# A new order for every engine of a clustered-attention and gated-FFN kernel, with some casts and copies on other engines and other PSUM banks

## The chip, the core and the metric

One core of a Trainium2 chip runs the whole kernel. The metric is the time of one execution on the device in microseconds (us); of several runs the median is given. The engines of the core are TensorE (PE, with its weight loads as PEld), VectorE (DVE), ScalarE (ACT), GpSimd (POOL) and SyncE (SP), which here only issues DMAs. Each engine works through its own queue in order.

## What is computed

Four batches, eight heads, 768 tokens, 64 columns a head. Each query and each key is given the cluster (of 16) whose normalized centroid it is closest to. A query attends only to the keys of its own cluster, and the output of the attention goes through a gated FFN with a convolution of three taps over the tokens:

```python
mask = q_assign[:, :, :, None] == k_assign[:, :, None, :]
scores = where(mask, scale * q @ k.T, -1e9)
x = softmax(scores) @ v                       # heads side by side: 4 x 768 x 512
h = maximum(x @ w_in, 0.0)                    # 1024 columns
conv_out = sum(conv_w[k] * hp[:, k:k + S, :] for k in range(3))
out = (h * sigmoid(conv_out)) @ w_out         # 4 x 768 x 512, float32
```

## The kernel before

The work is written as a list of some 1,680 short steps, the string `PLAN`. The function `step` (line 752) turns each into instructions, in the order of the list; no scheduler moves them afterwards. So the list fixes the order of every engine's queue, and a step waits on its engine until its operands are there and the buffers that it writes are free. A suffix such as `@2` names the PSUM bank that a matmul step writes: 0 to 3 are the four `flex` banks, 4 and 5 are the two halves of the score buffer `sc0` (used so only at the end).

The heads are taken in pairs, `g` = 0 to 15, four pairs to a batch. The attention runs in 32 slots `t`, one for a pair and half of its queries (384); a pair has two slots. The steps, by name:

- **Loads.** `L`, `LQ`, `LK`, `LZ`, `LV` load queries, keys and values (SP's queue; `La` on ACT's), `_wl` weights. Pairs 0 to 6 are transposed on PE (`T`, line 301) and copied out of PSUM by ACT (`Qa`) or DVE (`Qd`); pairs 7 to 15 are transposed in blocks on DVE (`Z`).
- **Casts to 16 bits.** `CD` (POOL), `CDd` (DVE), `CDa` (ACT) write queries and keys into `ext`, `CV` and `CVd` the values, `_wp`, `_wd`, `_wa` the weights. `_z` and `_zd` clear the other half of `ext`. They all go through `copy` (line 319), so most of them show as line 323 (POOL and DVE) or 321 (ACT).
- **Clusters.** `A` multiplies with the centroids (line 347), `M0` to `M6` find the best one on DVE (lines 364 to 389), `K` turns the result on PE, `B` copies it on DVE (line 406) and `BX` sends it by DMA into rows of `ext`, `BA` does so from ACT's queue (line 410). For pair 0 `KM` and `KCa`/`KCd` (line 423) write these rows by copies. With these rows the score matmul adds a large negative number where the clusters differ.
- **Attention.** `S.t.i` (i = 0 to 5) are two score matmuls of 384 columns into one of two score buffers (line 442). `E.t.i` is the exponential on ACT (line 454), 128x768. `V.t.u` (u = 0 to 5) are six matmuls that add up 128 rows of the result in a `flex` bank (line 466). `N.t` divides by the sum on DVE (lines 479 and 480). The result goes to `xT` by a DMA transpose (`XD`) or by PE and a copy (`X`, `Ya`, `Yd`).
- **FFN**, for units `n` = 0 to 31 (a batch, half of the tokens, two blocks of 128 columns). `I.n.f` are four matmuls (line 524), `Ra`/`Rd` the relu (lines 537 and 539), `C`/`Ca`/`Cd` carry three columns between the halves. The convolution is three steps `c`, `a`, `b` on DVE (lines 558 and 560), or `W` on PE into a score buffer (line 566) with the taps that `_ta`, `_td`, `_tp` make. `H` is the tanh (line 584), `G` the gate on DVE (line 592).
- **Output.** `O` are two, `U` one of the eight matmuls of a 128-row output tile (line 604), `Fa`/`Fd` empty the bank (lines 617 and 619), `FX` stores.
- **Set-up.** `_k` are three matmuls of zeros; `_id`, `_io`, `_n0` to `_n7d`, `_cw0` to `_cw2`, `_pk`, `_sd`, `_v`, `_hz` make constants.

Buffers rotate: four for query and key loads, four for value loads, six for `ext`, four for `attn`, two score buffers, two for `x16`, three for `hpad`, two each for the convolution and the tanh, four for outputs.

Of the kernel before, what the change touches and what calls it, by code (L numbers as in the profile page):

```python
# [871 lines left out]
```

## Time and profile before

| | |
|---|---|
| median of 3 runs (lowest to highest) | 241.73 us (241.42 to 241.91) |
| the profiled execution | 240.68 us |
| its span, first to last instruction | 238.9 us |
| granted TensorE clock, mean | 0.998 |
| idle of PE, DVE, ACT, POOL in the span | 11.2, 23.5, 23.5, 154.3 us |

A row of a group reads: line, engine, operation, out<-in with shapes, count, then busy us and mean ns of one, then the idle time of the engine just before them with what ended it. A row of the timeline reads: start and length in us, engine, line, operation, count, and in brackets the idle time before it and what ended it. A matmul's length holds the way through the array too, so the pace of a run of matmuls is read from their starts.

### The profile page before, as it was taken

To read this page: it belongs to the slowest core of one execution; us is meant where nothing else is said; L and a number is where in the kernel's file an instruction comes from. 1 tells how busy PE (TensorE), PEld (TensorE's weight loads), DVE (VectorE), ACT (ScalarE), POOL (GpSimd) and SP (SyncE) were. 2 spreads that over 40 slices of the span, in tenths; PEclk is the share of its full clock that TensorE was granted. 3 is DMA by queue.
4 is the path that set the end of the run, shared out by engine and by line. 5 is a ranking of instruction groups with operands and counts; after the bars stand their busy time and mean duration, and the time that the engine had idled before them with its cause. 6 is when DMAs were issued, how large, how long until landed. Compare 5 with 4: busy or idle time off the path is not lost.

```text
span 238.9 us, 6438 instructions
## 1 busy us (share of the span) xinstructions
PE 227.7 (95%) x2442; PEld 143.5 (60%) x2442; DVE 215.4 (90%) x497; ACT 215.4 (90%) x337; POOL 84.6 (35%) x149
## 2 busy tenths in 40 slices
...
GB/s 198 294 243 257 157 233 245 323 80 83 242 92 136 183 128 94 173 126 183 163 150 169 114 3 188 153 134 1 168 89 63 33 47 16 105 64 112 68 0 177
DMA packets 102958, 32.77 MB, mean 137 GB/s; under 512 B 94603, under 2 KB 98187, under 8 KB 102926
## 3 DMA queue, kind: packets, MB, share of 16 engines
...
q10 hardware_dynamic: 327, 0.24, 0.4%
...
## 4 chain that ended last, share of the span: by engine, by line
PE 64%; DVE 15%; ACT 12%; POOL 5%; issue 2%; DVEq 0%; POOLq 0%
PE sc L442 17%; PE flex L524 15%; PE flex L604 14%; PE flex L466 10%; ACT attn L454 8%; PE flex L347 3%; POOL ext L323 3%; PE sc L566 3%; ACT th L584 2%; DVE best L380 1%; DVE ext L323 1%; DVE cnv L560 1%; DVE x L480 1%; PE sc L604 1%; DVE val L377 1%
## 5 line engine op out<-in xcount | busy, mean ns | idle before, releaser
L454 ACT ACTIVATE attn<-sc 128x768 f16<-128x768 f32 x192 | 146.4, 817 | 4.0 <-PE sc L442 2.7
L442 PE MATMUL sc<-ext 128*128 128x384 f16 x384 | 89.3, 325 | 3.8 <-ACT attn L454 2.1
L466 PEld LDWEIGHTS <-attn 128*128 128x128 f16 x1152 | 50.5, 97 | 15.2 <-ACT attn L454 0.4
L560 DVE SCALAR_TENSOR_TENSOR cnv<-hpad,cwcol,cnv 128x382 f16<-128x382 f16 (+1 forms) x100 | 58.4, 609 | 0.4
L323 POOL CAST ext<-qkT 64x768 f16<-64x768 f32 x48 | 41.7, 875 | 40.6 <-DVE qkT L298 20.0
L466 PE MATMUL flex<-v,attn 128*128 128x65 f16 x1152 | 54.5, 193 | 0.3 <-ACT attn L454 0.3
L524 PE MATMUL flex<-xT,w_in 128*128 128x384 f16 x256 | 49.1, 326 | 0.1
L442 PEld LDWEIGHTS <-ext 128*128 128x128 f16 x384 | 32.5, 97 | 26.9 <-issue 9.2
L604 PE MATMUL flex<-w_out,hg 128*128 128x512 f16 x176 | 47.1, 379 | 0.0
L592 DVE SCALAR_TENSOR_TENSOR hg<-th,hpad 128x764 f16<-128x764 f32 (+2 forms) x33 | 30.7, 934 | 3.1 <-ACT th L584 3.0
L524 PEld LDWEIGHTS <-w_in 128*128 128x128 f16 x256 | 23.9, 98 | 15.6 <-issue 0.6
L604 PEld LDWEIGHTS <-hg 128*128 128x128 f16 x192 | 17.9, 98 | 16.8 <-DVE hg L592 1.1
L537 ACT ACTIVATE hpad<-flex 128x384 f16<-128x384 f32 x45 | 21.8, 501 | 2.4 <-PE flex L524 1.6
L323 POOL CAST v<-v_in 128x768 f16<-128x768 f32 x15 | 14.6, 977 | 24.7 <-DMA v_in<-in_v_dram 24.6
L584 ACT ACTIVATE th<-cnv 128x764 f32<-128x764 f16 (+1 forms) x25 | 21.2, 848 | 0.7 <-DVE cnv L560 0.7
L323 POOL COPY hpad<-hf 128x6 f16<-128x6 f16 x12 | 4.9, 418 | 42.0 <-DVE hg L592 41.8
L480 DVE TENSOR_TENSOR x<-flex,rec 128x384 f16<-128x384 f32 x32 | 17.8, 558 | 1.1
L298 DVE STREAM_TRANSPOSE qkT<-qk_in 128x768 f32<-128x768 f32 x18 | 17.3, 966 | 0.0
L558 DVE TENSOR_SCALAR cnv<-hpad,cwcol 128x382 f16<-128x382 f16 (+1 forms) x50 | 16.3, 349 | 0.6 <-ACT hpad L537 0.5
L323 POOL COPY hf<-hpad 128x6 f16<-128x6 f16 x11 | 3.6, 329 | 30.7 <-ACT hpad L537 18.6
L347 PE MATMUL flex<-qkT,cT 128*32 128x192 f32 x256 | 14.1, 333 | 0.0
L309 PE MATMUL flex<-id,qk_in 128*128 128x128 f32 x84 | 12.5, 287 | 1.2 <-ACT qkT L315 0.6
...
## 6 DMA issues: line engine op xcount, KB each, us to landing
...
```

Source lines behind the costliest of these rows:

```text
L323: (nc.vector if name == "d" else nc.gpsimd).tensor_copy(out=to, in_=src)
L347: nc.tensor.matmul(bank[at][32 * j : 32 * (j + 1), 192 * i : 192 * (i + 1)], lhsT=cT32[:, which, :], rhs=tokens[:, j], start=True, stop=Tr ...
L442: nc.tensor.matmul(s[:, n, 0:HS], lhsT=ext_b[g % NE][:, h, 1, P * (kt + n) : P * (kt + n + 1)], rhs=ext_b[g % NE][:, h, 0, HS * a : HS * ( ...
L454: nc.scalar.activation(attn[t, i // 3][:, kt : kt + 2, :], sc[(6 * t + i) % 2][:, :, 0:HS], AF.Exp, scale=0.125)
L466: nc.tensor.matmul(avp(at)[:, u, 0 : D + 1], lhsT=attn[t, h][:, kt, P * jq : P * (jq + 1)], rhs=v16_b[g % NE][:, h, kt, 0 : D + 1], start= ...
L480: nc.vector.tensor_tensor(out=x16[t].rearrange("p jq (h d) -> p h jq d", h=2), in0=av[:, :, 0:D].rearrange("p (h jq) d -> p h jq d", h=2), ...
L524: nc.tensor.matmul(bank[at][:, 0:HS], lhsT=w_in16[:, r, 2 * u + f, :], rhs=xT[:, b % 2, r, HS * a : HS * (a + 1)], start=(r == 0), stop=(r ...
L537: nc.scalar.activation(to, src, AF.Relu)
L560: nc.vector.scalar_tensor_tensor(out=cnv, in0=src, scalar=w, in1=cnv, op0=ALU.mult, op1=ALU.add)
L584: nc.scalar.activation(th_t[n][:, fs, 0:N], pre[:, fs, 0:N], AF.Tanh, scale=0.5)
L592: nc.vector.scalar_tensor_tensor(out=hg_b[b][:, 2 * u + fs.start : 2 * u + fs.stop, LO[a] : LO[a] + N], in0=th_t[n][:, fs, 0:N], scalar=1. ...
L604: nc.tensor.matmul(bank[at][:, 0:Dm], lhsT=hg_b[b][:, fb, P * tq : P * (tq + 1)], rhs=w_out16[:, fb, :], start=(fb == 0), stop=(fb == NFB ...
```

## The change

The list is laid out anew: each engine's order, the engine of some casts and copies, and the banks. The kinds and counts of all matmul steps stay, except that one `_k` (three matmuls of zeros) is gone. `KR = P` slices `ext` to the 128 partitions that it has.

The steps that differ in engine, by count (before, after): ACT: `CDa` 7, 8; `KCa` 2, 1; `Qa` 16, 15; `Ra` 45, 46; `Fa` 19, 16; `Ya` 3, 2; `_ta` 9, 8; `_wa` 4, 3. DVE: `CDd` 9, 6; `CVd` 1, 2; `KCd` 2, 3; `Qd` 7, 8; `Rd` 19, 18; `Fd` 5, 8; `Yd` 2, 3; `Cd` 7, 4; `_wd` 4, 3; `_zd` 4, 5. POOL: `CD` 48, 50; `CV` 15, 14; `C` 23, 26; `_tp` 10, 11; `_wp` 8, 10; `_z` 8, 7.

133 lines of the list go and 133 come. Here are its beginning, places in the middle and its end, and the two other edits:

```diff
@@ -15,140 +15,140 @@
...
-    "LQ.0.0 _id _io _zero _k.10@2 _zd.5.0 _k.17@3 _zd.3.0 _zd.3.1 _pk.4 _sd _z.0.1 _k.14@1 _hz.1 _z.1.1 "
-    "_cent _n1 _z.1.0 _z.0.0 _hz.2 _pk.0 _v.1 _z.2.1 _pk.2 _pk.1 _z.4.0 T.0.0@2 La.0.0 T.0.1@1 _n0 _nq _n2 "
-    "_n5 _id16 _zd.4.1 _n3@3 _n4@3 Qa.0.0 Qa.0.1 CDd.0.0.1 CDa.0.0.0 LK.0.1 T.0.3@2 Qa.0.3 A.0.0@3 M0.0.0 "
-    "M1.0.0 M2.0.0 M3.0.0 _cw0 LQ.0.1 T.0.2@1 Qa.0.2 CDa.0.1.1 LQ.1.0 T.1.0@0 _cw1@2 _cw2 _tp.20 Qa.1.0 "
-    "A.0.1@1 M4.0.0 M0.0.1 M1.0.1 M5.0.0 M2.0.1 M6.0.0 M3.0.1 LK.1.0 T.1.1@3 Qa.1.1 _ta.10 CDd.1.0.0 LQ.1.1 "
-    "T.1.2@1 Qa.1.2 LK.1.1 T.1.3@0 A.1.0@2 M0.1.0 M1.1.0 Qa.1.3 CD.1.1.1 _ta.6 _td.22 KM.0.0.1@1 KCa.0.0.1 "
-    "KM.0.0.0@3 KCd.0.0.0 M4.0.1 M2.1.0 M3.1.0 M4.1.0 A.1.1@2 M0.1.1 M5.1.0 M5.0.1 M6.1.0 M6.0.1 M1.1.1 "
-    "_z.5.1 CDa.0.1.0 S.0.0 "
-    "E.0.0 L.2 T.2.0@0 Qa.2.0 T.2.2@1 Qa.2.2 T.2.1@3 Qa.2.1 CD.2.1.1 CD.1.1.0 CD.1.0.1 S.0.1 E.0.1 _n7d "
-    "M2.1.1 M3.1.1 M4.1.1 _v.0 _pk.3 CD.2.0.0 S.0.2 _tp.19 K.1.0@1 B.1.0 KM.0.1.0@2 KCd.0.1.0 E.0.2 "
-    "CDa.2.1.0 A.2@3 M0.2 M1.2 KM.0.1.1@1 KCa.0.1.1 CD.2.0.1 _tp.21 M5.1.1 _td.8 M6.1.1 M2.2 _k.3@0 L.3 "
-    "T.3.0@2 Qa.3.0 T.3.1@0 Qa.3.1 CDd.3.0.1 M3.2 _z.2.0 T.3.2@1 Qa.3.2 CD.3.1.1 CD.3.0.0 _v.3 CD.3.1.0 "
-    "S.0.3 E.0.3 S.0.4 E.0.4 K.1.1@0 B.1.1 BA.1.1 _ta.7 M4.2 M5.2 M6.2 L.4 T.4.2@3 T.4.0@2 T.4.1@1 S.0.5 "
-    "E.0.5 Qa.4.0 Qd.4.2 Qd.4.1 A.3@0 M0.3 LV.0 CV.0 BX.1.0 S.1.0 S.1.1 "
...
-    "S.4.0 T.6.1@0 Qd.6.1 V.2.5@2 K.5@3 S.4.1 "
...
-    "E.9.0 A.8@2 M0.8 N.6 S.9.2 E.9.1 E.9.2 M1.8 B.7 M2.8 S.9.3 E.9.3 V.9.0@2 S.9.4 V.9.1@2 V.9.2@2 LZ.9.0 "
-    "BX.6 LZ.9.1 Z.9.0 H.2 G.2 E.9.4 S.9.5 E.9.5 CV.4 V.8.0@1 V.8.1@1 V.8.2@1 V.8.3@1 V.8.4@1 S.10.0 "
...
-    "E.18.3 V.17.4@0 V.17.5@0 O.1.0.0@1 E.18.4 a.13.1 Rd.14.1 M4.13 N.17 b.13.1 a.12.1 a.13.0 M5.12 M5.13 "
...
-    "CV.10 V.18.0@1 V.18.1@1 O.1.1.0@3 S.19.4 V.18.2@1 V.18.3@1 M6.13 H.12 G.12 M6.12 E.19.4 V.19.0@0 S.19.5 "
...
+    "_zero _hz.2 _pk.0 _cent _zd.2.0 _zd.2.1 _z.4.1 _k.14@3 _sd _z.0.0 _id _z.1.0 _k.17@1 _k.10@3 _zd.0.1 "
+    "La.0.0 LQ.0.0 T.0.0@1 _n0 _n1 _nq _n2 _n3@2 _n5 _n4@2 T.0.1@3 Qa.0.0 Qd.0.1 _id16 CDd.0.0.1 LK.0.1 "
+    "T.0.3@2 Qa.0.3 LQ.0.1 T.0.2@0 Qa.0.2 CDa.0.0.0 A.0.0@3 M0.0.0 M1.0.0 M2.0.0 _io A.0.1@0 M0.0.1 M1.0.1 "
+    "M3.0.0 _n7d M4.0.0 M2.0.1 M5.0.0 CDa.0.1.1 LK.1.1 T.1.3@3 LQ.1.0 T.1.0@2 Qa.1.0 LK.1.0 T.1.1@1 Qa.1.1 "
+    "_pk.1 _z.5.0 CDa.0.1.0 _cw0 _cw1@2 _cw2 _tp.11 LQ.1.1 T.1.2@1 Qa.1.2 Qa.1.3 CD.1.1.0 _tp.19 M6.0.0 "
+    "KM.0.0.0@2 M3.0.1 M4.0.1 M5.0.1 A.1.0@0 M0.1.0 KCd.0.0.0 M6.0.1 M1.1.0 M2.1.0 KM.0.0.1@1 KCa.0.0.1 "
+    "CD.1.0.1 _z.3.1 A.1.1@0 M0.1.1 M3.1.0 M1.1.1 M4.1.0 M2.1.1 M5.1.0 M3.1.1 M4.1.1 _td.16 M6.1.0 CDa.1.1.1 "
+    "S.0.0 "
+    "E.0.0 L.2 T.2.0@3 Qa.2.0 T.2.2@0 Qa.2.2 KM.0.1.0@1 KCd.0.1.0 T.2.1@2 Qa.2.1 CD.2.0.1 _pk.4 _v.0 "
+    "CD.2.1.1 CD.2.0.0 S.0.1 E.0.1 KM.0.1.1@3 KCd.0.1.1 A.2@0 CDd.1.0.0 M5.1.1 S.0.2 S.0.3 K.1.0@1 B.1.0 "
+    "CDa.2.1.0 _pk.2 E.0.2 E.0.3 M0.2 M1.2 M2.2 M6.1.1 M3.2 _z.3.0 L.3 T.3.2@3 T.3.0@1 T.3.1@2 Qa.3.0 Qa.3.1 "
+    "CD.3.0.0 S.0.4 E.0.4 S.0.5 K.1.1@1 Qa.3.2 CD.3.1.1 CD.3.1.0 CD.3.0.1 _zd.1.1 B.1.1 BA.1.1 L.4 T.4.0@2 "
+    "Qd.4.0 T.4.1@0 M4.2 T.4.2@1 Qd.4.2 E.0.5 Qa.4.1 _ta.7 A.3@2 M0.3 M1.3 M5.2 M2.3 M6.2 LV.0 BX.1.0 S.1.0 "
...
+    "E.3.0 T.6.1@2 Qd.6.1 S.3.2 E.3.1 E.3.2 X.0@1 S.3.3 T.6.2@0 S.3.4 E.3.3 _wl.0 K.4@2 LV.2 CVd.2 V.2.0@3 "
+    "E.3.4 S.3.5 E.3.5 Yd.0 Qd.6.2 M3.5 M4.5 B.4 M5.5 V.2.1@3 V.2.2@3 _td.5 M6.5 _wd.14 S.4.0 V.2.3@3 S.4.1 "
+    "E.4.0 V.2.4@3 S.4.2 E.4.1 E.4.2 CDd.6.0.1 K.5@0 V.2.5@3 N.2 B.5 S.4.3 A.6@1 M0.6 _wp.0 _tp.2 S.4.4 "
...
+    "E.9.1 V.8.0@1 S.9.2 V.8.1@1 V.8.2@1 V.8.3@1 V.8.4@1 S.9.3 E.9.2 E.9.3 V.8.5@1 N.8 S.9.4 S.9.5 E.9.4 "
+    "E.9.5 V.9.0@3 V.9.1@3 S.10.0 V.9.2@3 "
...
+    "c.14.1 V.17.4@0 V.17.5@0 N.17 G.12 c.13.1 S.19.2 E.19.2 _ta.12 O.1.1.0@2 O.1.1.1@2 LV.11 LZ.14.1 S.19.3 "
+    "V.18.0@0 V.18.1@0 S.19.4 V.18.2@0 E.19.3 E.19.4 I.15.0@3 Ra.15.0 C.15 S.19.5 V.18.3@0 V.18.4@0 E.19.5 "
...
-    "E.20.0 V.19.2@0 O.1.1.1@3 V.19.3@0 S.20.1 S.20.2 V.19.4@0 XD.17 XD.18 V.19.5@0 N.19 XD.19 FX.0.3 FX.1.0 "
...
-    "V.20.0@1 V.20.1@1 S.21.1 V.20.2@1 "
...
-    "S.31.4 O.2.2.3@3 V.31.2@0 Fd.2.2 FX.2.2 E.31.3 FX.2.4 Cd.27 S.31.5 E.31.4 O.3.0.0@2 O.3.0.1@2 E.31.5 "
-    "O.3.1.0@3 V.31.3@0 V.31.4@0 V.31.5@0 O.3.1.1@3 O.3.0.2@2 O.3.0.3@2 N.31 X.31@0 Ya.31 _ta.14 O.3.1.2@3 "
-    "O.3.1.3@3 Fa.3.1 FX.3.1 Fd.3.0 FX.3.0 I.28.0@2 I.28.1@0 Ra.28.0 Rd.28.1 I.29.1@3 I.30.0@1 Ra.30.0 "
-    "I.29.0@2 Cd.28 W.28.0@1 W.28.1@1 Ra.29.0 Rd.29.1 C.26 Cd.30 c.30.0 a.30.0 b.30.0 H.28 G.28 C.25 C.29 "
-    "I.30.1@2 Ra.30.1 c.30.1 I.31.0@1 Rd.31.0 a.30.1 b.30.1 W.29.0@1 W.29.1@1 H.29 G.29 H.30 G.30 I.31.1@3 "
-    "U.3.5.0@0 U.3.5.1@0 U.3.3.0@5 U.3.3.1@5 U.3.2.0@4 C.31 W.31.0@1 U.3.4.0@1 U.3.2.1@4 U.3.3.2@5 U.3.3.3@5 "
-    "U.3.2.2@4 U.3.2.3@4 Ra.31.1 U.3.5.2@0 W.31.1@1 H.31.0 G.31.0 H.31.1 U.3.4.1@1 U.3.2.4@4 U.3.3.4@5 "
-    "U.3.4.2@1 U.3.3.5@5 U.3.2.5@4 U.3.2.6@4 G.31.1 U.3.2.7@4 Fa.3.2 FX.3.2 U.3.3.6@5 U.3.3.7@5 Fa.3.3 "
-    "FX.3.3 U.3.5.3@0 U.3.5.4@0 U.3.5.5@0 U.3.5.6@0 U.3.5.7@0 U.3.4.3@1 U.3.4.4@1 U.3.4.5@1 U.3.4.6@1 Fa.3.5 "
-    "FX.3.5 U.3.4.7@1 Fa.3.4 FX.3.4 "
...
+    "V.19.2@1 V.19.3@1 S.20.4 V.19.4@1 V.19.5@1 E.20.4 S.20.5 E.20.5 Ra.15.1 FX.1.0 XD.17 FX.0.5 LZ.15.0 "
+    "XD.18 N.19 XD.19 LV.14 A.14@3 S.21.0 V.20.0@1 S.21.1 Fd.1.1 V.20.1@1 V.20.2@1 "
...
+    "O.2.2.3@3 V.31.2@0 S.31.5 O.3.0.0@2 O.3.0.1@2 O.3.0.2@2 E.31.5 V.31.3@0 V.31.4@0 V.31.5@0 N.31 _tp.0 "
+    "O.3.1.0@1 O.3.1.1@1 O.3.1.2@1 X.31@0 Yd.31 O.3.1.3@1 Fa.3.1 O.3.0.3@2 Fd.3.0 Cd.27 XD.30 I.28.0@0 C.26 "
+    "Rd.28.0 C.28 I.28.1@1 Rd.28.1 FX.3.0 FX.3.1 Fd.2.2 FX.2.2 FX.2.4 I.30.0@2 W.28.0@1 W.28.1@1 H.28 G.28 "
+    "I.29.0@1 Ra.29.0 I.29.1@0 Ra.29.1 Rd.30.0 Cd.30 c.30.0 a.30.0 I.30.1@3 Ra.30.1 c.30.1 a.30.1 b.30.1 "
+    "b.30.0 C.25 Ca.29 I.31.0@1 Ra.31.0 I.31.1@0 Ra.31.1 U.3.2.0@4 W.29.0@1 W.29.1@1 H.29 U.3.3.0@5 "
+    "U.3.5.0@0 U.3.5.1@0 U.3.3.1@5 C.31 U.3.4.0@2 U.3.2.1@4 W.31.0@1 U.3.4.1@2 W.31.1@1 G.29 U.3.2.2@4 "
+    "U.3.5.2@0 U.3.5.3@0 U.3.3.2@5 U.3.2.3@4 H.30 G.30 H.31.0 H.31.1 G.31.0 U.3.3.3@5 U.3.3.4@5 U.3.3.5@5 "
+    "U.3.3.6@5 U.3.4.2@2 G.31.1 U.3.3.7@5 U.3.2.4@4 U.3.2.5@4 U.3.2.6@4 U.3.2.7@4 Fd.3.3 FX.3.3 U.3.5.4@0 "
+    "U.3.5.5@0 Fd.3.2 FX.3.2 U.3.5.6@0 U.3.5.7@0 Fa.3.5 FX.3.5 U.3.4.3@2 U.3.4.4@2 U.3.4.5@2 U.3.4.6@2 "
+    "U.3.4.7@2 Fa.3.4 FX.3.4 "
...
@@ -180,6 +180,7 @@
     SPB = 2 * NPR
     NU = 2 * NPR
     BR = 3
+    KR = P
     SHARP = 24.0
 
 
@@ -441,8 +442,8 @@
         for n in range(2):
             nc.tensor.matmul(
                 s[:, n, 0:HS],
-                lhsT=ext_b[g % NE][:, h, 1, P * (kt + n) : P * (kt + n + 1)],
-                rhs=ext_b[g % NE][:, h, 0, HS * a : HS * (a + 1)],
+                lhsT=ext_b[g % NE][0:KR, h, 1, P * (kt + n) : P * (kt + n + 1)],
+                rhs=ext_b[g % NE][0:KR, h, 0, HS * a : HS * (a + 1)],
                 start=True,
                 stop=True,
             )
```

203 rows, old and new, of the table PLAN are left out of this document.

## The prediction

> **What bounds the kernel now.** I read the busy times first, then the same in four stretches, then the matmul queue in order of time, then the idle times of ScalarE (ACT).
>
> ```profile
> PE 227.7 (95%) x2442; PEld 143.5 (60%) x2442; DVE 215.4 (90%) x497; ACT 215.4 (90%) x337; POOL 84.6 (35%) x149
> ...
> 0.00:23.00 23.00, 20.19 (x185) 13.76 (x186) 20.23 (x62) 18.92 (x34) 15.89 (x48) 1.00 0.89 247
> 23.00:73.00 50.00, 46.17 (x601) 30.67 (x601) 47.50 (x113) 47.68 (x74) 27.11 (x42) 1.00 0.76 183
> 73.00:216.00 143.00, 142.72 (x1545) 89.59 (x1544) 137.66 (x305) 139.45 (x215) 41.40 (x60) 1.00 0.52 111
> 216.00:239.00 23.00, 18.60 (x114) 9.51 (x112) 9.97 (x19) 9.35 (x17) 0.19 (x1) 0.98 0.25 92
> ```
>
> Columns of a stretch: PE, weight loads, DVE, ACT, POOL. Three engines are nearly full, so the question is who waits for whom. The matmul queue tells (start, length):
>
> ```profile
> 170.56 0.81 PE L442 MATMUL sc<-ext 128*128 128x384 f16 x4
> 171.21 0.54 PE L466 MATMUL flex<-v,attn 128*128 128x65 f16 x12
> 171.59 0.81 PE L524 MATMUL flex<-xT,w_in 128*128 128x384 f16 x4
> 172.24 0.49 PE L442 MATMUL sc<-ext 128*128 128x384 f16 x2
> ```
>
> Starts follow each other by 0.65 (four matmuls of 384), 0.38 (twelve of 65) and 0.65 us: nothing waits. From 73 to 216 us PE is busy 142.72 of 143 in this way, so it sets the pace there, and what it does not have to do in that stretch, or has begun earlier, comes off the end. Ahead of 73 us PE idles and ACT (47.68 of 50) sets the pace: scores have two buffers, and a pair of score matmuls waits until the exponential two before it is through. So the sum is: how much earlier is ACT at the last exponential of slot 9 (about 73 us), what has PE left to do from there, what new waits interrupt it, and the tail.
>
> **The change part by part.** By engine I counted each plan's steps. PE issues the same matmuls, less one group of three zero matmuls (`_k.3`, which filled an idle stretch: nothing). The slice `0:KR` is the whole tile: nothing. ACT loses 3 evacuations, 1 rows copy, 1 chunk copy, 1 xT copy, 1 tap and 1 weight cast and gains 1 cast and 1 relu:
>
> ```profile
> L321 ACT ACTIVATE ext<-qkT 64x768 f16<-64x768 f32 x7 | 5.9, 842 | 0.1
> L321 ACT ACTIVATE ext<-flex 3x768 f16<-3x768 f16 x2 | 1.6, 801 | 0.1
> L315 ACT ACTIVATE qkT<-flex 128x384 f32<-128x384 f32 x8 | 3.6, 477 | 0.1
> L745 ACT ACTIVATE taps<-id,cwcol 128x128 f16<-128x128 f16 x9 | 3.5, 402 | 0.9 <-DVE pack L389 0.9
> L321 ACT ACTIVATE w_in<-w_sb 128x512 f16<-128x512 f32 x2 | 1.1, 620 | 0.0
> L537 ACT ACTIVATE hpad<-flex 128x384 f16<-128x384 f32 x45 | 21.8, 501 | 2.4 <-PE flex L524 1.6 <-DVE hg L592 0.2
> L617 ACT ACTIVATE o_sb<-flex 128x512 f32<-128x512 f32 x17 | 10.3, 606 | 1.2 <-PE flex L604 1.0
> L497 ACT ACTIVATE xT<-flex 128x384 f16<-128x384 f16 x3 | 1.5, 495 | 2.5 <-PE flex L491 2.5
> ```
>
> That is 3 x 606 + 801 + 477 + 495 + 402 + 620 - 842 - 501 = 3.27 us less on ACT over the kernel. Ahead of slot 9's last exponential the same rows give: minus 801, 477, 402, 620, plus 842 and two relus (1002), less one 0.2 carry: **0.7 us less** (a).
>
> The start (b). The first scores wait for DVE's copy of the bias rows:
>
> ```profile
> 12.38 0.56 DVE L323 COPY ext<-flex 3x768 f16<-3x768 f16 x1
> ...
> 12.99 0.48 PE L442 MATMUL sc<-ext 128*128 128x384 f16 x2 [0.78 <-DVE ext L323]
> ...
> L323 DVE CAST ext<-qkT 64x768 f16<-64x768 f32 x9 | 5.5, 610 | 0.2
> ```
>
> Between the first argmax step and that copy the new order takes a cast (`CDd.1.0.0`, 0.61), a small reduction and a tap out of DVE's queue, and puts another small reduction and two copies of a few columns in (`_n7d`): about **0.5 us earlier** (0 to 0.8).
>
> The ACT-issued bias transfer of pair 1 (c). `BA.1.1` waits on ACT's queue for DVE's `B.1.1`, and holds what is behind it while it issues:
>
> ```profile
> 20.98 0.21 DVE L406 COPY spk<-flex 36x128 f16<-36x128 f16 x1
> ...
> 21.22 1.37 ACTq L410 DMA_DIRECT2D ext<-spk  x1
> 22.64 0.40 ACT L745 ACTIVATE taps<-id,cwcol 128x128 f16<-128x128 f16 x1 [0.93 <-DVE pack L389]
> ...
> L716 DVE MEMSET ext<- 64x768 f32 x4 | 2.8, 698 | 0.6 <-issue 0.4
> ```
>
> Behind it stand now a tap and the last exponential of slot 0, and in the new order that exponential, a copy and the tap. New ACT arrives 0.5 (start) and 0.8 (the rows copy, which went to DVE) earlier, at 20.4 instead of 21.7. But `B.1.1` now stands behind a memset (0.70) and that rows copy, for a cast and a tap that left: I take it 0.4 us later, 21.4, and the issue ends 1.4 later, 22.8. So ACT idles 2.4 us here instead of 0.93: **1.5 us lost** (ends: 0, if DVE is as early as ACT; 2.0, if all that was added counts). The lead of the start is gone by 23 us.
>
> The stop at slot 4 (d):
>
> ```profile
> 38.48 0.48 PE L442 MATMUL sc<-ext 128*128 128x384 f16 x2
> 39.25 0.66 PE L309 MATMUL flex<-id,qk_in 128*128 128x128 f32 x4 [0.28 <-DVE xT L499]
> ...
> 40.53 0.22 PE L401 MATMUL flex<-id,pack 128*128 128x128 f16 x1 [0.43 <-DVE qkT L317]
> 40.59 0.81 PE L442 MATMUL sc<-ext 128*128 128x384 f16 x4
> ...
> 41.11 4.56 ACT L454 ACTIVATE attn<-sc 128x768 f16<-128x768 f32 x6 [1.23 <-PE sc L442]
> ```
>
> `S.4.1` stands behind `T.6.1` and `K.5`, which both wait for DVE to empty a bank, and ACT starves 1.23 us. In the new order only one value group (0.19 us) stands between `S.4.0` and `S.4.1`, and `K.5` comes after `S.4.2`: **1.2 us won**. Sum at slot 9: -0.7 - 0.5 + 1.5 - 1.2 = -0.9 us.
>
> PE's rest (e). Ahead of `S.9.5` the new order has six value groups of slot 8 where the old has three of slot 9: three groups of six matmuls more, 3 x 0.19 = **0.6 us** less left. From there to `S.31.5` and to the end both issue the same matmuls.
>
> Banks (f). Value groups of neighbouring slots use the same bank five times (1-2, 14-15, 15-16, 17-18, 19-20), before twice. Then the next group waits until DVE's normalization has read the bank.
>
> ```profile
> L480 DVE TENSOR_TENSOR x<-flex,rec 128x384 f16<-128x384 f32 x32 | 17.8, 558 | 1.1
> L479 DVE RECIPROCAL rec<-flex 128x6 f32<-128x6 f32 x32 | 5.8, 180 | 3.3 <-PE flex L466 3.1
> L592 DVE SCALAR_TENSOR_TENSOR hg<-th,hpad 128x764 f16<-128x764 f32 x16 | 15.3, 962 | 1.0 <-ACT th L584 1.0
> L560 DVE SCALAR_TENSOR_TENSOR cnv<-hpad,cwcol,cnv 128x382 f16<-128x382 f16 x52 | 29.9, 607 | 0.1
> ...
> 68.58 0.79 PE flex L347 x16
> ```
>
> The tight ones are 17-18 (two score pairs and two output steps lie between, 2 x 0.33 + 4 x 0.216 = 1.5 us) and 19-20 (two score pairs and an assignment, 0.66 + 0.79 = 1.45). The bank is free 0.2 (matmul to read) + x + 0.74 us after the last value matmul, x being what DVE still has in front. With one gate (0.96) in front, each stalls 0.4: I take **0.6 us** in all; 0 if DVE is on time.
>
> The tail (g). Now:
>
> ```profile
> 230.52 1.41 PE L604 MATMUL sc<-w_out,hg 128*128 128x512 f16 x4
> 231.97 0.60 ACT L617 ACTIVATE o_sb<-sc 128x512 f32<-128x512 f32 x1 [1.23 <-PE sc L604]
> 232.62 0.59 PE L604 MATMUL sc<-w_out,hg 128*128 128x512 f16 x2 [0.69 <-ACT o_sb L617]
> 233.05 2.32 PE L604 MATMUL flex<-w_out,hg 128*128 128x512 f16 x10
> ```
>
> Ten output matmuls in a row take 2.32, the last one's result some 0.16 of it: 0.216 each, 0.86 for four. The four at 230.52 are followed 2.10 later: 0.26 on the last gate and the rest on the evacuation of `sc`'s other half, 1.2 us. In the new tail both halves are filled before either is read, and the last gates have four to eight matmuls in front: this stall goes. A new one stands at `W.28.0`, behind a relu (549 ns on DVE) and `C.28`, which moves from DVE to POOL (a POOL carry of this kind is 418 ns by its group): 0.2 to 0.8, I take 0.6. Net **0.6 won** (0.4 to 1.0).
>
> POOL gets 3.3 us more (2 casts, 3 carries, 1 tap, 2 weight casts, less a memset and a value cast), in 40 us of idle time: nothing.
>
> ```profile
> L323 POOL CAST ext<-qkT x48: 815/820/1391, 11.5 to 169.4; 64x768 f16<-64x768 f32 x48
> ```
>
> The row's longest cast is 0.57 us over its median. The Trainium skill (GPSIMD Engine Reference, Key points) says that GpSimd shares its SBUF interfaces with VectorE and contends with instructions of two SBUF inputs. The spread agrees; by that rule the sum would be some 0.6 us worse where a cast stands right ahead of its scores (`CD.14.0.1` and `S.26.0`), by the median it stays.
>
> **Sum:** -0.9 - 0.6 + 0.6 - 0.6 = -1.5 us. The profiled execution took 240.68, 1.05 under the median of 241.73; so 239.2 for its like, and **240.2** as median (238.7 to 240.7 by the ends of c; f without stalls takes 0.6 off, g at its lower end adds 0.2).
>
> **The rivals.** *DVE is late with the banks (slower).* If a gate and two taps (0.96 + 2 x 0.61 = 2.18) stand ahead of the normalization at 17-18 and 19-20, each stalls 0.2 + 2.18 + 0.74 - 1.47 = 1.65: -2.1 (the sum without f) + 3.3 = +1.2, **242.9**. It decides from x = 1.6 us (2.1 / 2 - 0.2 - 0.74 + 1.47). For it: DVE is 96% busy there. Against: in the old order PE waits nowhere there.
>
> *The stop at slot 4 returns (no change).* `CVd.2` brings a value cast from POOL to DVE; its load leaves the SP queue behind `BX.3` and a weight load of 768 KB.
>
> ```profile
> POOL v L323 <- DMA v_in<-in_v_dram: 24.6, 6, 10.3
> ```
>
> POOL waited 24.6 us for such loads at no cost; on DVE a wait holds `V.2.0` and the scores behind it. If it costs what d wins, -0.3: **241.4**.
>
> *ACT is the bound throughout.* Then all of its 3.27 us come off: **238.5**. The Trainium skill (Perfetto Trace Analysis, Identifying the Most-Contended Engine) says to judge TensorE by the share of weight loads and not of matmuls: 60% here, against 90% on ACT, which gives this time. The back-to-back starts speak against it after 73 us.
>
> That the change is not what it says, I exclude: the counts agree with it.
>
> **How the numbers follow.** Forecast 0.46, ACT 0.13, slot 4 0.17, banks 0.24. Within 0.2% (0.5 us) is what a measurement here cannot tell from no change. Faster: 0.46 + 0.13 + 0.03 of slot 4 = 0.62; same: 0.14 of slot 4 + 0.02 of banks = 0.16; slower 0.22. The range reaches from under the ACT case, by c's lower end with f's, to the bank case: 238.0 to 243.0.
>
> **What would show it.** First exponential near 13.0; ACT idle some 2.4 us ahead of the last exponential of slot 0; no wait near `S.4.1`; PE over 99% busy after 73 us, with short waits at `V.18.0` and `V.20.0`; no wait of PE for an evacuation near 231 us, and one ahead of `W.28.0`. It is wrong if PE's waits after 73 us sum to over 2 us, or if ACT is not earlier at slot 9.

## The result, and the profile after

The new order is slower: 244.79 us median of 20 runs (241.84 to 247.57) against 241.09 of 20 runs of the kernel before (240.33 to 244.48), a ratio of 1.0117, 95% interval 1.0092 to 1.0142. Ratios here leave out runs over 1.5% above the fastest of the same kernel, six of these 20, so that the ratio of the medians is higher, 1.0153. The profiled execution of the new order took 244.31 us with a span of 242.5, 3.6 more than before.

Columns as in the prediction. First the whole of the new order, then three stretches of 10 us in which TensorE (PE) loses, then the same stretches before:

```profile
PE 227.1 (94%) x2439; PEld 142.7 (59%) x2439; DVE 221.6 (91%) x497; ACT 212.8 (88%) x331; POOL 87.5 (36%) x155
...
20.00:30.00 10.00, 7.25 (x69) 4.28 (x68) 9.60 (x22) 6.58 (x12) 6.46 (x16) 1.00 0.69 201
60.00:70.00 10.00, 8.10 (x94) 5.29 (x93) 9.96 (x22) 9.26 (x15) 1.53 (x2) 1.00 0.89 162
90.00:100.00 10.00, 8.74 (x139) 6.10 (x136) 9.90 (x24) 8.72 (x14) 3.54 (x6) 1.00 0.60 100
```
```profile
20.00:30.00 10.00, 8.86 (x113) 6.26 (x112) 9.63 (x27) 9.07 (x16) 7.68 (x10) 1.00 0.75 223
60.00:70.00 10.00, 9.18 (x115) 5.57 (x112) 9.57 (x21) 9.72 (x15) 2.62 (x4) 1.00 0.76 181
90.00:100.00 10.00, 9.91 (x159) 7.16 (x159) 9.72 (x26) 9.46 (x15) 4.43 (x7) 1.00 0.67 124
```

PE and ACT lose together (1.61 and 2.49 us in the first of them), while DVE, busy 6.2 us longer than before (221.6 against 215.4), is nearly full in all three. How far the new order is behind, by the ends of the same exponential in both traces: 0.18 us at E.0.0, 1.17 at E.0.5, 2.79 at E.1.5, 4.06 at E.3.5, 2.74 at E.4.1, 3.70 at E.8.0, 3.55 at E.9.5, 5.17 at E.13.5, 4.66 at E.31.5, 3.6 at the end. So 2.8 us are lost by 33 us, some 2 more by 102, and the tail gives 1.0 back. These are single traces, one of each kernel.

**The first 30 us.** The start, in the new order:

```profile
13.09 1.00 DVE L374 TENSOR_TENSOR eqq<-sim,mx 128x192 f16<-128x192 f32 x1
...
13.05 0.82 POOL L324 CAST ext<-qkT 64x768 f16<-64x768 f32 x1
...
14.63 0.55 PE L310 MATMUL flex<-id,qk_in 128*128 128x128 f32 x3 [0.84 <-DVE sim L365]
...
12.82 0.84 ACT L322 ACTIVATE ext<-qkT 64x768 f16<-64x768 f32 x1
13.69 0.81 ACT L455 ACTIVATE attn<-sc 128x768 f16<-128x768 f32 x1
```

The first scores end at 13.35, but the cast `CDa.1.1.1`, now on ACT, stands in front of the exponential until 13.67. Of the 1.17 us at E.0.5, 0.96 are lost right behind it, between E.0.0 and E.0.1: `M2.1.0` on DVE takes 1.00 (0.35 in the order before) beside a POOL cast, so `M0.1.1` empties its bank only at 14.58, and PE waits 0.84 ahead of `T.2.2`. This wait, 0.80 to 0.85, stands in the traces of all ten variants below too, r1 to r10; no run took it out. Then pair 1's second cluster rows, by DVE, ACT's queue, SP's queue and PE:

```profile
21.72 0.70 DVE L717 MEMSET ext<- 64x768 f32 x1 [0.22 <-issue]
22.45 0.22 DVE L407 COPY spk<-flex 36x128 f16<-36x128 f16 x1
...
25.33 0.91 DVE L387 TENSOR_SCALAR pack<-best 128x24 f16<-128x24 f32 x1
26.53 0.86 DVE L390 SCALAR_TENSOR_TENSOR pack<-best,pack 128x12 f16<-128x12 f32 x2
...
22.70 1.36 ACTq L411 DMA_DIRECT2D ext<-spk  x1
24.10 0.81 ACT L455 ACTIVATE attn<-sc 128x768 f16<-128x768 f32 x1 [1.58 <-DVE best L381]
29.68 0.81 ACT L455 ACTIVATE attn<-sc 128x768 f16<-128x768 f32 x1 [1.60 <-PE sc L443]
...
20.51 0.38 SPq L259 DMA_DIRECT2D qk_in<-in_q_dram  x1
...
22.18 0.48 SPq L280 DMA_DIRECT2D v_in<-in_v_dram  x1
...
27.54 0.22 PE L402 MATMUL flex<-id,pack 128*128 128x128 f16 x1 [0.62 <-POOL pack L713]
29.14 0.50 PE L443 MATMUL sc<-ext 128*128 128x384 f16 x2 [1.39 <-DMA ext<-spk]
```

`B.1.1` ends at 22.66, 1.47 later than before. ACT then issues the DMA (`BA.1.1`) until 24.06, and the rows reach `ext` only at 29.1: 5 us, behind 1.9 MB of loads (pair 5 and weights, 768 KB each, and values, 384) that left SP's queue from 20.5 to 22.7. `S.1.3` waits 1.39 us for them and ACT behind it 1.60. The M5 and M6 steps of DVE (0.91 and 0.86) hold `K.2` too; an M5 takes 0.17 elsewhere. In the order before:

```profile
17.62 0.39 SPq L258 DMA_DIRECT2D qk_in<-in_q_dram  x1
...
18.85 0.52 SPq L642 DMA_DIRECT2D w_sb<-in_moe_w_out_dram  x1
...
26.28 0.87 PE L442 MATMUL sc<-ext 128*128 128x384 f16 x4
```

Pair 5 and the weights had left by 19.4 (the values followed at 25.5), `BA.1.1` was through at 22.59, and `S.1.3` started at 26.28 without a wait.

**Slot 4**, by DVE, PE and ACT:

```profile
41.04 0.56 DVE L324 CAST v<-v_in 128x768 f16<-128x768 f32 x1 [0.79 <-DMA v_in<-in_v_dram]
...
41.66 0.36 PE L467 MATMUL flex<-v,attn 128*128 128x65 f16 x6 [0.80 <-DVE v L324]
...
42.38 0.81 ACT L455 ACTIVATE attn<-sc 128x768 f16<-128x768 f32 x1 [0.73 <-PE sc L443]
```

The stop ahead of `S.4.1` is gone, and `CVd.2` on DVE waits for its load: ACT idles 0.73 ahead of `E.3.5` instead of 1.23 ahead of `E.4.1`.

**62 to 67 us**, DVE and PE:

```profile
62.05 0.89 DVE L390 SCALAR_TENSOR_TENSOR pack<-best,pack 128x12 f16<-128x12 f32 x2
64.47 1.81 DVE L593 SCALAR_TENSOR_TENSOR hg<-th,hpad 128x764 f16<-128x764 f32 x2
66.20 0.55 DVE L540 TENSOR_SCALAR hpad<-flex 128x384 f16<-128x384 f32 x1
...
66.81 0.22 PE L402 MATMUL flex<-id,pack 128*128 128x128 f16 x1 [0.93 <-DVE hpad L540]
```

`K.7` waits until the relu `Rd.3.0` has emptied its bank, behind two gates. **92 us**, DVE, POOL and PE of the new order, then DVE and POOL of the kernel r3 (below), in which these steps stand in the same order:

```profile
92.14 2.00 DVE L559 TENSOR_SCALAR cnv<-hpad,cwcol 128x386 f16<-128x386 f16 x3
...
92.31 1.70 POOL L324 CAST ext<-qkT 64x768 f16<-64x768 f32 x2 [4.06 <-PE sc L443]
...
95.07 0.53 PE L348 MATMUL flex<-qkT,cT 128*32 128x192 f32 x8 [0.69 <-DVE qkT L299]
```
```profile
92.23 0.78 DVE L543 TENSOR_SCALAR cnv<-hpad,cwcol 128x386 f16<-128x386 f16 x3
...
92.99 1.70 POOL L308 CAST ext<-qkT 64x768 f16<-64x768 f32 x2 [2.43 <-PE sc L427]
```

The same three taps take 2.00 us when a POOL cast has begun just ahead of the second of them (92.31; `c.6.0` at 92.37) and 0.78 when they come first and the cast after. The 1.2 us go on to the transpose behind them and to `A.10`, which waits for it. **The tail** is as foretold, and a little better: `W.28.0` (first of the six) and the output matmuls show no wait:

```profile
225.52 1.15 PE L567 MATMUL sc<-hpad,taps 128*128 128x386 f16 x6
...
235.61 1.24 PE L605 MATMUL sc<-w_out,hg 128*128 128x512 f16 x5
236.69 2.11 PE L605 MATMUL flex<-w_out,hg 128*128 128x512 f16 x9
```

### The profile page after: what moved, and what is told of

Its sections match the earlier page's. It is cut to its first block, busy times and chain, and to the rows that moved or that the text cites. A ratio compares the mean times of both kernels' runs of the same rounds, so it can differ in the third digit from the quotient of the medians.

```text
span 242.5 us, 6404 instructions
## 1 busy us (share of the span) xinstructions
PE 227.1 (94%) x2439; PEld 142.7 (59%) x2439; DVE 221.6 (91%) x497; ACT 212.8 (88%) x331; POOL 87.5 (36%) x155
## 4 chain that ended last, share of the span: by engine, by line
PE 61%; DVE 21%; ACT 8%; DMA 5%; issue 3%; SPq 1%; DVEq 0%; ACTq 0%
PE sc L443 16%; PE flex L605 14%; PE flex L525 13%; PE flex L467 9%; ACT attn L455 6%; DMA ext<-spk 3%; DMA v_in<-in_v_dram 2%; PE sc L567 2%; PE flex L348 2%; DVE cnv L561 2%; DVE qkT L299 2%; DVE eqq L374 2%; DVE sim L365 2%; PE flex L310 1%; PE sc L605 1%
## 5 line engine op out<-in xcount | busy, mean ns | idle before, releaser
L324 POOL CAST ext<-qkT 64x768 f16<-64x768 f32 x50 | 45.0, 901 | 53.7 <-DVE qkT L299 24.2
L467 PEld LDWEIGHTS <-attn 128*128 128x128 f16 x1152 | 49.4, 97 | 14.9 <-DVE v L324 1.1
L467 PE MATMUL flex<-v,attn 128*128 128x65 f16 x1152 | 53.2, 193 | 0.8 <-DVE v L324 0.8
L605 PE MATMUL flex<-w_out,hg 128*128 128x512 f16 x176 | 46.1, 379 | 0.0
L538 ACT ACTIVATE hpad<-flex 128x384 f16<-128x384 f32 x46 | 22.6, 507 | 1.0 <-PE flex L525 0.3
L324 POOL COPY hpad<-hf 128x6 f16<-128x6 f16 x12 | 3.7, 311 | 37.7 <-PE flex L525 19.0
L324 POOL CAST v<-v_in 128x768 f16<-128x768 f32 x14 | 12.2, 874 | 12.6 <-DMA v_in<-in_v_dram 12.4
L324 POOL COPY hf<-hpad 128x6 f16<-128x6 f16 x14 | 5.5, 393 | 29.8 <-ACT hpad L538 25.4
L618 ACT ACTIVATE o_sb<-flex 128x512 f32<-128x512 f32 x16 | 9.8, 613 | 6.7 <-PE flex L605 6.7
```

Source lines behind the costliest of these rows:

```text
L324: (nc.vector if name == "d" else nc.gpsimd).tensor_copy(out=to, in_=src)
L467: nc.tensor.matmul(avp(at)[:, u, 0 : D + 1], lhsT=attn[t, h][:, kt, P * jq : P * (jq + 1)], rhs=v16_b[g % NE][:, h, kt, 0 : D + 1], start= ...
L538: nc.scalar.activation(to, src, AF.Relu)
L605: nc.tensor.matmul(bank[at][:, 0:Dm], lhsT=hg_b[b][:, fb, P * tq : P * (tq + 1)], rhs=w_out16[:, fb, :], start=(fb == 0), stop=(fb == NFB ...
```

## The experiments

Theory 1: the rows, which land late, are the loss of the start. Theory 2: DVE instructions that begin while a POOL cast runs are held until it ends, and this is the rest. Rival: PE or DVE is slowed by many small waits, and none is worth much alone. Diffs are in steps of the list.

| kernel | median us (range) | before, same runs | ratio, 95% interval |
|---|---|---|---|
| r1_rows_early | 244.24 (243.44 to 245.88) | 241.28 | 1.0116 [1.0073, 1.0158] |
| r2_loads_later | 244.93 (243.78 to 245.98) | 241.28 | 1.0131 [1.0088, 1.0174] |
| r4_pool_order | 245.25 (241.96 to 246.28) | 241.28 | 1.0103 [1.0043, 1.0162] |
| t1_new_tail | 240.31 (239.49 to 242.78) | 241.28 | 0.9962 [0.9924, 1.0000] |
| r5_rows_from_sp | 243.09 (242.01 to 244.78) | 241.17 | 1.0080 [1.0050, 1.0109] |
| r3_values_earlier | 244.37 (241.94 to 245.07) | 241.17 | 1.0107 [1.0073, 1.0141] |
| r7_turn_bank | 244.64 (243.88 to 245.72) | 241.17 | 1.0136 [1.0094, 1.0178] |
| p1_pool_casts | 245.93 (one run) | 241.17 | |
| r6_rows_both_pairs | 242.40 (241.40 to 243.81) | 241.32 | 1.0042 [1.0009, 1.0075] |
| t2_slot4_only | 241.09 (240.44 to 244.29) | 241.32 | 0.9982 [0.9951, 1.0013] |
| t3_slot4_and_tail | 240.11 (239.27 to 242.81) | 241.32 | 0.9953 [0.9909, 0.9996] |
| r8_rows_and_pool | 242.63 (241.50 to 243.92) | 241.12 | 1.0046 [1.0022, 1.0070] |
| r9_turn_later | 242.16 (241.47 to 243.79) | 241.12 | 1.0027 [0.9996, 1.0057] |
| r10_relu_first | 242.32 (241.46 to 244.17) | 241.76 | 1.0025 [0.9996, 1.0054] |

**Pair 1's rows, first try.**

```diff
+ L.3 L.4 LV.0 K.1.0@1 B.1.0 M5.1.1 M6.1.1 K.1.1@1 ... M0.2 B.1.1 BX.1.0 BX.1.1   (ahead of T.3.2)
- BA.1.1   (and M5.1.1 M6.1.1 K.1.1@1 B.1.1 BX.1.0 at their old places)
```

> The new order, in which DVE finds pair 1's second cluster rows (M5, M6), PE turns them and DVE copies them (B.1.1) right behind the first ones, and their DMA leaves from SP's queue ahead of the 1.9 MB of loads (pair 5, a weight load, values of pair 1) instead of from ACT's queue. Theory 1 (this DMA, landing behind those loads, is the loss of the first 30 us): S.1.3 no longer starts at 29.1 us but when its score buffer is free, about 27; PE's stalls between 20 and 30 us fall from 4.7 to about 2; 244.8 falls to 242 to 242.8. Rival (many small waits, the rows only the one that shows): another wait takes its place, under 0.5 us gained, 244.3 or more.

244.24: nothing gained, though `S.1.3` has no wait any more. The edit was badly made: the memset of the second half of pair 1 now comes after its rows, waits for their DMA and clears them (so that head is computed without them), `K.1.1` makes PE wait 1.4 us for `M6.1.1`, and DVE, held by the memset, brings `K.2` 1.1 later. It tells only that these waits are exchanged for one another when DVE is late.

**The loads behind pair 2's rows.**

```diff
- _wl.4 ... LV.1 CV.1 BX.2 S.2.0
+ BX.2 LV.1 _wl.4 CV.1 S.2.0
```

> The new order, in which only two loads (the weights of 768 KB and the values of pair 1, 384 KB) and the value cast leave later: behind the rows of pair 2 in SP's queue. The late copy B.1.1 and ACT's issue stay. If the rows land late because of the bytes in front of them, S.1.3 starts about 1.5 to 2 us earlier and the time falls by 1 to 2 us, 243 to 243.8. If only DVE's lateness counts, S.1.3 stays at 29 us and the time at 244.8 or above, as the values of pair 1 are later now.

In its trace `S.1.3` has no wait, although `B.1.1` ends as late (22.81): 1.1 MB less in front of the rows brought them in time, so it is the bytes and not only DVE's lateness. The time did not fall, because the values of pair 1 are then late (PE idles 1.66 us ahead of `V.1.0`) and those of pair 2 (2.11 at `V.2.0`): the loads are needed just as soon.

**The rows from SP's queue.**

```diff
- _zd.1.1 B.1.1 BA.1.1 ... LV.0 BX.1.0
+ _z.1.1   (POOL, behind _z.3.1) ... B.1.1 ... LV.0 BX.1.0 BX.1.1
```

> The new order with two steps on other engines: the memset of the second half of pair 1 runs on POOL at about 15 us (idle there) instead of on DVE at 21.7, and the rows of pair 1's second head leave from SP's queue right behind the first ones, ahead of the loads of pair 5, weights and values (1.9 MB), instead of from ACT. Theory 1: B.1.1 ends about 0.7 to 1 us earlier (21.7 to 22.0), ACT's last exponential of slot 0 starts about 1.5 earlier than 24.1, S.1.3 has no wait for a DMA; PE's stalls between 20 and 30 us fall from 4.7 to 2.5 or less, 242 to 243.3. Rival (DVE, behind with the argmax steps, sets the pace there): K.2 waits as before and S.1.3 is hardly earlier; 244 or more.

243.09, by the ratios 0.37% (0.9 us) less than the new order. `S.1.3` has no wait, and the next rows take its place, those of pair 2 (row below): `B.2` is nearly as late as in the new order (it ends at 27.6 against 28.0), and its DMA goes out behind the same loads, now later.

```profile
33.18 0.82 PE L427 MATMUL sc<-ext 128*128 128x384 f16 x4 [2.31 <-DMA ext<-spk]
...
32.00:34.00 2.00, 0.82 (x10) 0.57 (x11) 1.93 (x7) 0.28 (x1) 1.42 (x2) 1.00 0.93 231
34.00:36.00 2.00, 2.00 (x29) 1.25 (x25) 0.64 (x2) 1.82 (x3) 1.94 (x6) 0.59 0.84 225
36.00:38.00 2.00, 2.00 (x20) 0.82 (x19) 0.15 (x1) 1.03 (x2) 1.84 (x4) 0.55 0.94 281
```

The third number from the end is the granted clock, and here it shows a second price of the wait: 0.59 and 0.55 for 4 us after it, that is (0.41 + 0.45) x 2 = 1.7 us of clock lost, on top of the wait.

**The rows of both pairs.**

```diff
  r5_rows_from_sp and r3_values_earlier, and
- Qd.4.2 ... A.3@2 M0.3 M1.3 M5.2 M2.3 M6.2 ... S.1.0 ... S.1.2 K.2@3 B.2 ... L.5 ... _wl.4 ... LV.1 CV.1 BX.2
+ Qd.4.2 M5.2 M6.2 ... A.3@2 M0.3 M1.3 ... S.1.0 K.2@3 B.2 M2.3 ... L.5 BX.2 ... LV.1 CV.1 _wl.4
```

> r5_rows_from_sp and r3_values_earlier together, and the same for pair 2: DVE's M5.2 and M6.2 ahead of the next chunk's steps, K.2 on PE behind S.1.0, its rows in SP's queue behind the load of pair 5 and ahead of the values of pair 1, and the weights of 768 KB behind these. Theory 1, now with pair 2 in it (in r5_rows_from_sp the wait of S.1.3 for a DMA went and S.2.0 stood 2.5 us for the rows of pair 2): neither S.1.3 nor S.2.0 waits for a DMA, PE's stalls between 20 and 40 us fall from 5.5 (changed kernel) and 6.5 (r5) to under 4, as in the order before (3.4); 241.2 to 242.2. Rival (the early stretch is only one of many losses, or a new wait comes): 242.7 or more.

242.40 and a ratio of 1.0042 against 1.0117: 1.8 us of the 2.8 are back. The time lies between what theory 1 foretold (242.2 at most) and its rival (242.7 or more). The longest wait of a score matmul for rows in its trace is 0.2 us, and none of its 12 runs had a lowered clock (mean granted clock 0.997 or more). Of the 20 runs of the new order 10 had one (0.984 to 0.993, median 245.70) and 10 not (median 243.98); of r3's 12 runs 10 had one, of r5's 12 runs 7, of the kernel before none in over 100. So the rows seem to cost twice: by the wait, and in half of the runs by a lowered clock, with 1.7 us more of time. How much of the 1.7 is the clock is not shown, since the wait differs too from run to run: `S.1.3` waits 0.63 us in r4's trace, 1.39 in the new order's, 2.12 in r7's. Theory 1 stands for most of the loss; the 1.8 us also hold a memset that went from DVE to POOL and the earlier values (r3, below, at most a few tenths).

**Pair 2's values earlier.**

```diff
- BX.3 S.3.0 ... _wl.0 K.4@2 LV.2 CVd.2
+ LV.2 BX.3 S.3.0 ... _wl.0 K.4@2 CVd.2
```

> The new order with the load of pair 2's values ahead of the rows of pair 3 and of the 768 KB of weights in SP's queue, issued at about 30 instead of 35.5 us. Theory (the wait of CVd.2 on DVE for this load takes the place of the stop at slot 4): the stall of PE ahead of V.2.0 (0.97 us, ACT then idle 0.6 ahead of E.3.5) goes, 0.4 to 0.9 us gained, 243.9 to 244.4. Rival (DVE and ACT are behind there anyway): under 0.2.

The wait at `V.2.0` is gone in the trace. 244.37, ratio 1.0107: within the interval of the new order, so at most a few tenths by the ratios. The 0.4 to 0.9 that it was expected to gain are not shown.

**POOL's order near 92 us.**

```diff
- CD.10.0.0 ... CD.9.1.0 ... CD.10.1.0
+ CD.9.1.0 ... CD.10.1.0 CD.10.0.0
```

> The new order with one step moved on POOL alone: the cast CD.10.0.0 goes behind CD.9.1.0 and CD.10.1.0, so that no POOL cast runs when DVE comes to the taps c.6.0 and c.6.1. Theory 2 (a DVE instruction of these kinds that begins while a POOL cast runs is held until the cast ends): c.6.0 and c.6.1 take 0.32 instead of 0.88 and 0.96 us, Z.10.1 ends 1.2 earlier, the second half of A.10 has no wait (0.89 now) and K.8 less (0.73 now): 243.6 to 244. Rival (they are long for a reason of their own): they stay at 0.9, 244.8.

In its trace `c.6.0` and `c.6.1` take 0.32 each, and PE is busy 9.93 of the 10 us from 90 to 100 instead of 8.74, as theory 2 says. The median, 245.25 of 6 runs, five of them with a lowered clock, tells nothing: this kernel still has the wait for rows. r8 repeats it without:

```diff
  r6_rows_both_pairs and r4_pool_order
```

> r6_rows_both_pairs with the POOL order of r4_pool_order (CD.10.0.0 behind CD.9.1.0 and CD.10.1.0). If the rows and the held DVE instructions near 92 us are what is left of the loss: c.6.0, c.6.1 and M5.9 take 0.32, 0.32 and 0.17 us in every run, PE's stalls between 90 and 100 us fall from 1.9 to 0.4 or less, the highest times go, and the median is 241.0 to 241.6, within 0.2% of the kernel before. Rival (the stall near 93 us is paid back later, or it is not in most runs): 242.2 or more, as in r6.

242.63, ratio 1.0046: as r6, and as its rival says. In r6's trace the taps were held (PE busy 8.67 from 90 to 100), in r8's not (9.82), and the medians are equal. The held taps are shown, but a loss of the median by them is not: of the seven traces in which the list is the same there (the new order, r1, r2, r3, r5, r6, r7) only two, the new order's and r6's, have them. What they cost where they come, the traces do tell: from the start of `S.9.5` to that of `S.31.5` it is 143.4 and 143.6 us in these two, 141.8 to 142.0 in those of the nine other variants r1 to r10, and 142.9 in the order before. So the hold takes some 1.5 us from a run in which it falls.

**Casts on POOL beside DVE's work.**

```diff
  in the kernel before, behind C.19
+ 12 times: gpsimd.tensor_copy(out=ext_b[4][0:D, 0, 0, :], in_=qkT[15][0:D, 0, :])
```

> The order before with twelve more POOL casts (64x768, float32 to float16, of data that nobody reads afterwards) behind C.19, from about 179 to 189 us, where POOL was idle and DVE's steps all took their shortest time (c 0.31, a and b 0.61, G 0.95, Cd 0.17). Theory 2: the steps c and Cd that begin while a cast runs are held until it ends, so take 0.4 to 0.9 us; whether a, b and G (two inputs in SBUF) are held too is what this run shows. If they are: DVE loses some 5 us between 179 and 189 and PE waits; if not, 2 us. Rival (no lock, the long ones have other reasons): all keep their lengths.

DVE from 180 us on in the kernel before, then DVE and POOL in this one:

```profile
180.15 0.94 DVE L592 SCALAR_TENSOR_TENSOR hg<-th,hpad 128x764 f16<-128x764 f32 x1
181.01 1.01 DVE L539 TENSOR_SCALAR hpad<-flex 128x384 f16<-128x384 f32 x2
182.05 0.56 DVE L323 CAST ext<-qkT 64x768 f16<-64x768 f32 x1
182.64 0.55 DVE L558 TENSOR_SCALAR cnv<-hpad,cwcol 128x386 f16<-128x386 f16 x2
183.17 1.15 DVE L560 SCALAR_TENSOR_TENSOR cnv<-hpad,cwcol,cnv 128x386 f16<-128x386 f16 x2
```
```profile
180.81 1.57 DVE L577 SCALAR_TENSOR_TENSOR hg<-th,hpad 128x764 f16<-128x764 f32 x1
182.30 1.01 DVE L524 TENSOR_SCALAR hpad<-flex 128x384 f16<-128x384 f32 x2
183.34 1.01 DVE L308 CAST ext<-qkT 64x768 f16<-64x768 f32 x1
184.39 1.65 DVE L543 TENSOR_SCALAR cnv<-hpad,cwcol 128x386 f16<-128x386 f16 x2
186.03 2.28 DVE L545 SCALAR_TENSOR_TENSOR cnv<-hpad,cwcol,cnv 128x386 f16<-128x386 f16 x2
...
180.35 10.62 POOL L723 CAST ext<-qkT 64x768 f16<-64x768 f32 x10
```

The gate takes 1.57 instead of 0.94, the cast 1.01 instead of 0.56, two `c` 1.65 instead of 0.55, two `a` or `b` 2.28 instead of 1.15: 0.45 to 0.63 each. The relu, which reads PSUM, keeps its 1.01 for two. POOL pays too, 1.06 a cast against 0.82 alone. The loss goes through to the end: this execution is 5.25 us longer than the profiled one before, 4.7 of them lost between E.25.5 and E.29.5. Theory 2 holds, for instructions of one and of two inputs in SBUF. The Trainium skill (SBUF — State Buffer, SBUF: two separate sides) describes it as an exclusive lock that whoever starts first holds for its whole instruction; the rows here agree.

**The bank of K.7, and the relu ahead of the gates.**

```diff
- K.7@3 ... K.6@2
+ K.7@2 ... K.6@3
```

> The new order with only two banks exchanged: K.7 on bank 2 and K.6 on bank 3. In the new order K.7 waits for Rd.3.0, which empties bank 3 on DVE behind two gates and a transpose. If that wait holds the scores of slot 8: the stall of 1.09 ahead of K.7 goes and E.8.0 follows E.7.5 without its idle time of 0.65; 0.6 to 0.9 gained, 244.0. If ACT or DVE sets the pace there the stall moves on to S.8.0 or later and nothing is gained, 244.8.

The stall at `K.7` went and one of 0.73 ahead of `A.8` came (DVE's `B.7` is as late as before): 244.64, nothing gained. Next, the turn of pair 2 later, and then `Rd.3.0` moved on DVE:

```diff
  r8_rows_and_pool, and
- S.1.0 K.2@3 B.2 M2.3 ... S.1.1 A.4@0
+ S.1.0 ... S.1.1 A.4@0 K.2@3 B.2 M2.3
```

> r8_rows_and_pool with K.2 on PE behind S.1.1 and A.4 instead of behind S.1.0, where it waited 1.35 us for DVE's M6.2 and held the scores. ACT sets the pace there (its idle time ahead of E.1.1 is 0.9 us in r6): 0.5 to 1.0 us less than r8. If DVE, behind with the argmax steps, sets the pace, the wait comes back at S.2.0 or K.3 and nothing is gained.

242.16, ratio 1.0027, 0.5 us better than r8, the intervals overlap; no verdict alone.

```diff
  r9_turn_later, and
- H.0 G.0 G.1 I.3.0@3 Rd.3.0
+ H.0 I.3.0@3 Rd.3.0 G.0 G.1
```

> r9_turn_later with the relu Rd.3.0 ahead of the two gates on DVE (it stood behind them), so that bank 3, which K.7 waits for, is empty about 1.9 us earlier. If that wait is the rest of the loss: the stall of 1.09 us ahead of K.7 goes, E.8.0 follows E.7.5 at once, 0.6 to 0.9 us less than r9, 241.2 to 241.6, within 0.2% of the kernel before. Rival (as in r7_turn_bank, where the stall went from K.7 to A.8): no gain, 242 or more.

Here unit 3's relu overwrites the buffer of unit 0 before its gate reads it, so that gate is computed from other values; the work is the same. `K.7` has no wait, but 242.32 with the same ratio as r9: another relu waits for the gate (ACT, below), as it needs the buffer.

```profile
65.69 0.49 ACT L522 ACTIVATE hpad<-flex 128x384 f16<-128x384 f32 x1 [0.58 <-DVE hg L577]
```

DVE is full there; in r9:

```profile
60.00:70.00 10.00, 8.09 (x99) 5.32 (x98) 10.00 (x22) 9.27 (x15) 1.52 (x2) 1.00 0.87 160
```

That DVE is the bound of this stretch fits both runs, in which exchanging who waits for it gained nothing; no run took work off it.

**The tail alone, and slot 4 alone,** in the kernel before.

```diff
t1: before up to S.31.3, then the new order
t2, in the order before:
- S.4.0 T.6.1@0 Qd.6.1 V.2.5@2 K.5@3 S.4.1 E.4.0 S.4.2
+ S.4.0 V.2.5@2 S.4.1 T.6.1@0 Qd.6.1 E.4.0 S.4.2 K.5@3
t3: both
```

> The order before up to S.31.3, and from there the new order. By the prediction's step on the tail the stop of 1.2 us at the evacuation near 231 us goes and a wait ahead of W.28.0 of 0.2 to 0.8 comes: 0.4 to 1.0 us faster than before, 240.1 to 240.7. By the trace of the changed kernel, which has no wait at either place, 1.1 to 1.2 faster, 239.9 to 240.0.

> The order before with only the stop at slot 4 taken out: S.4.1 comes right behind S.4.0 and one value group, T.6.1 behind it and K.5 behind S.4.2. By the prediction's step d the 1.23 us of idle time of ACT ahead of E.4.1 go and the kernel ends up to 1.2 us earlier, 240.0 to 240.4. Rival (the time comes back at the next evacuation, since T.6.1 and K.5 now wait in front of S.4.2 and S.4.3): under 0.5 gained, 240.7 or more.

> The order before with the edit of t2_slot4_only and the new order from S.31.3 on. If the two gains add, 239.0 to 239.4, the fastest of all; if the first is given back before the end, that of the new tail alone, 240.0 to 240.3.

The tail: 240.31 against 241.28, 0.4% (0 to 0.8), as foretold; by the traces of t1 and t3 1.02 us are won behind E.31.5. Slot 4: `E.4.1` ends 1.25 us earlier, `E.4.3` and what follows only 0.34, since `A.6` now holds `S.4.3`, waiting for the copy `Qd.6.1`; from E.27.3 on nothing of it is left in this trace, and the median shows no gain clear of noise (0.9951 to 1.0013):

```profile
40.99 0.86 PE L331 MATMUL flex<-qkT,cT 128*32 128x192 f32 x16 [0.40 <-DVE qkT L301]
...
42.38 4.36 ACT L438 ACTIVATE attn<-sc 128x768 f16<-128x768 f32 x6 [1.00 <-PE flex L385]
```

The stop moved by two exponentials. t3, 240.11, has the lowest median (0.9953, 0.9909 to 0.9996), not to be told from t1's.

## Why the prediction was wrong

It said 240.2 (238.0 to 243.0), faster at 0.62; it is 244.79.

- **(c) is the step that failed.** It asked who waits behind `BA.1.1` on ACT's queue and priced that (1.5 lost; measured 1.58 idle against 0.93, so 0.65, as ACT itself came at 22.5 and not at 20.4). It did not ask who waits for what the DMA brings. `S.1.3` does, and the rows need 5 us from the end of their issue behind 1.9 MB of loads; the copy was 1.47 later, not 0.4, because `M0.2`, `M1.2` and `B.1.0` (1.33 us), ahead of `M5.1.1` in the order before, now stand between it and the copy. The rows of pair 2 had the same fault (`B.2` 3.4 later) and no place in the sum. r6 gives 1.8 us for both, with a memset moved to POOL.
- **(b)** 13.0 foretold, 13.69 measured, 13.52 before. The scores were 0.14 earlier; the cast that came to ACT's queue ahead of the exponential took that and more. DVE's queue was followed, ACT's not. Right behind it came the 0.84 ahead of `T.2.2`, which is in no term of the sum.
- **(a)** 3.27 us of ACT's work were to go, 2.6 went (215.4 to 212.8). It was worth nothing: ACT was starved, and 3.55 late at slot 9, where 0.9 early was foretold.
- **(d)** The stop went as said, but 0.34 of its 1.23 us outlast the slot, by t2, and none the kernel: an engine's idle time that is moved past one wait meets the next. And the rival's wait came too, `CVd.2` for its load, 0.80 us on PE; r3 shows that it is worth little more in the end, for the same reason.
- **(e)** fits, but not in this trace: from the start of `S.9.5` to that of `S.31.5` the lag grows by 0.47 (4.19 to 4.66), with the held taps at 92 us in between. In the nine traces without these it shrinks by 0.9 to 1.1; 0.6 was foretold.
- **(f)** 0.6 foretold at `V.18.0` and `V.20.0`, none measured. The rival's mechanism, DVE late with a bank, came at `K.7`, where it was not looked for.
- **(g)** right, at the upper end: 1.0 won (the lag is 4.66 at E.31.5 and 3.64 at the end), no wait at `W.28.0`.
- **Held DVE instructions** were named in the prediction, but as longer POOL casts at one place and 0.6 us. It is DVE's side that counts: its instructions that are over 0.1 us longer than usual (than the shorter quarter of their step and form) sum to 7.3 us too much before and 12.2 after, and all of them, 23 before and 28 after, run beside a POOL instruction. Part of it lies in front of `T.2.2`, `K.2`, `K.7` and `A.10`.

It also said that it is wrong if ACT isn't earlier at slot 9; that is what happened. What stays open: after r9 the new order is still 0.3% (0 to 0.6) behind with a tail worth 0.4%, so some 0.7% are lost ahead of the tail. In r9's trace most of it comes in slots 1 to 3: the exponentials end 0.3 us earlier than before at E.0.5, 2.5 later at E.2.5, 3.4 at E.3.5, 2.2 at E.7.5, 2.8 at E.9.5. ACT waits there 0.65, 0.52 and 1.01 us ahead of E.1.4, E.2.2 and E.3.0, and no run tried these waits one by one. The stretch from 60 to 70 us, where DVE is full, adds only 0.6 of the 2.8; r7 and r10 didn't free it.
